# Top-32 attention into a mixture of experts: a drain planned anew between the last score tile and the first expert product

## The chip, the cores and the metric

One core of one Trainium2 chip runs the whole program. The metric is device microseconds of one execution; lower is better. Before the change the median of three runs is 365.16 us (362.47 to 365.77).

## The reference

```python
scores = scale * q @ k.T                      # 2 batches, 8 heads, 576 tokens, width 64
kth    = 32nd largest of each row
attn   = softmax(scores where scores >= kth, else -1e9) @ v
x      = attn as (1152, 512)                  # N = 1152 tokens
logits = x @ w_gate                           # 8 experts
e, gate_w = argmax(logits), softmax(logits)[e]
# each expert takes its tokens in order, up to its capacity of 288
out    = gate_w * (relu(x @ w1[e]) @ w2[e])   # 512 -> 1024 -> 512, a row of each token
```

## The kernel before

**Units.** The attention goes over 36 units u = 0 to 35: unit u = 4t + p is pair p of heads (two heads) of tile t of 128 tokens; there are nine tiles, t = 0 to 8. In the code L = 35 is the last unit and T = 8 the last tile. `attention` (L1041) is a pipeline written out by hand: in pass i it runs `heads(i)`, and steps of older units at fixed distances behind it.

**Steps of one unit.** `scores` (L292, PE) writes the scores into three PSUM banks. `heads` (L310, VectorE, called DVE) takes the eight largest of each of 16 segments, `merge` joins them, and `bound` (L346 to L350, three short DVE operations that depend on one another) makes a threshold from them. `shift` (L356, ScalarE, called ACT) copies the scores to SBUF. `sign` (L365, ACT) marks what is above the bound and counts it; `turn` (L372, mostly GpSimd, called POOL) multiplies the marks in; `select` (L393 to L400, DVE) finds the 32nd value; `penalty` (L409 ACT, L411 DVE) makes what is below it very small; `probs` (L428, L429 on PE, the exponential L430 on ACT) transposes and exponentiates; `values` (L450, L453, PE) multiplies by v; `normalise` (L464 to L469, DVE) divides, for two units at a time.

**Routing of a tile.** `route(t, stage)`: stage 0 transposes x (L516), 0.5 copies it out of PSUM (L520, L522), 1 makes the logits (L525), 1.5 splits x in two 16-bit halves (L528 to L534), 2, 2.1, 2.2 copy the logits (L536), find the largest and its index, 3 counts places (L545, L546), 3.5, 4, 5 work out slot and weight, 5.5 writes the tokens to `xbuf` in HBM by an indirect DMA of POOL (L559). The last tile has its stages 0 to 1 in two halves (0, 0.5, 1 and 0.1, 0.6, 1.1).

**Experts during the attention.** The first 128 tokens of the two experts first chosen ("a" and "b") are computed ahead. For "a" the hidden layer comes in four `quarter_h` (L657) with `quarter_take` (L704) and `quarter_split` (L708, L709), and the second product in four `quarter`s: each makes 128 of the 512 output columns with 24 matmuls (L757) and copies them out (L720). `split_w` cuts float32 weights in a 16-bit high part (part 0 or 2, L612, L616) and a low part (part 1, L618). Weights and loads live in 13 rotating SBUF buffers; one is taken again when the last reader of its tile is done.

**The drain.** After pass 34, L1124 to L1237 list by hand what is left, one list for all engines: each engine works through its own entries in that order, and waits where one is not ready. After the tokens of tile 8 are in `xbuf`, SyncE (called SP) loads them by transposing DMAs: `load_rest` (L648, L651) the rest of "a" and "b", `load_x(2)`, `load_x(3)` (L640) the next two experts. Then `experts` (L902) runs `ffn_rest` (first products L773) and the other six experts. Weights of 1 MB a piece are loaded by `load_w` (L603) on the same SP queue as the tokens; the scatters go through POOL's software queue.

Of the kernel before, what the change touches and what calls it, by code (L numbers as in the profile page):

```python
# [34 lines left out]
def kernel(  # L35
# [339 lines left out]
    def sign_turn(u, act, pool, turns=True):  # L375
        sign(u, (0,))
        for f, *a in act:
            f(*a)
        sign(u, (1,))
        if turns:  # L380
            turn(u, js=(0,))
        for f, *a in pool:
            f(*a)
        if turns:
            turn(u, js=(1,))
# [27 lines left out]
    def probs(u, *steps):  # L413
# [5 lines left out]
        for step in (0,) if whole else steps:  # L419
            if whole:  # L420
                bs, pt = range(9), P["p3", 0].tile([128, 9, 128], FT, name="p3", bufs=1)
            elif step < 2:
                bs, pt = range(5 * step, 5 * step + 4), bank4()
            else:
                bs, pt = (4,), (pv if TAIL_P else P["pt", 0].tile([128, 512], FT, name="ex", bufs=1))[:, None, 384:512]
# [269 lines left out]
    def quarter_h(c, a):  # L695
        if a == 0:
            Q["p"] = bank4()
        h_of(Q["p"][:, a], 0, 2 * c + a, "a")
# [12 lines left out]
    def quarter_y(c, a):  # L711
        if a == 0:
            Q["p"] = bank4()
        for k in (0, 1) if a == 0 else (2, 3):
            small_y("a", 0, Q["p"][:, 0], slice(128 * c, 128 * c + 128), k < 2, k % 2)

    def quarter_out(c):
        if c == 0:
            Q["y"] = work.tile([128, Dm], FT, name="y", tag="nat", bufs=4)
        nc.scalar.activation(Q["y"][:, 128 * c:128 * c + 128], Q["p"][:, 0], AF.Copy, scale=XE["a"][:, 0, 0:1])  # L720

    def quarter(c):
        quarter_y(c, 0)
        quarter_y(c, 1)
        quarter_out(c)
# [274 lines left out]
    def check(step):  # L1000
        if step == 1:
            pf = bank1()
# [14 lines left out]
    def count():  # L1017
        pc = bank1()
# [28 lines left out]
    def attention(side, early, late, mid, pads, act, pool, end):  # L1047
# [5 lines left out]
        for i in range(NU - 1):  # L1053
# [46 lines left out]
            run(at(4, values, 0) + picks + at(-1, scores) + at(4, values, 1) + routes((1, 1.5, 3)) + routes((0, 3.5)))  # L1100
# [8 lines left out]
            if last:  # L1109
                values(i - 3)  # L1110
# [20 lines left out]

        penalty(L - 3)
        bound(L - 1, 0)
        select(L - 2, 0)
        bound(L - 1, 1)
        select(L - 2, 1)
        bound(L - 1, 2)
        select(L - 2, 2)
        sign_turn(L - 1, act.get(L, []), [], False)
        run(pool.get(L, []))  # L1140
        probs(L - 3, 0, 1, 2)
        pad = [(lambda: None,)]
        small += [(select, L - 2, 3), (select, L - 2, 4)] + rt(T - 2, 2.1) + pad + rt(T - 2, 2.2) + [(turn, L - 1)]
        small += [(penalty, L - 2, (0,))] + 2 * pad + [(normalise, L - 4, st) for st in range(3)]
        heads(L, fill)
        drop()
        run(side.get(L, []))
        shift(L)
        penalty(L - 2, (1,))
# [6 lines left out]
        probs(L - 2, 0, 1, 2)  # L1156
        for st in range(3):
            bound(L, st)
        sign(L)
        run(rt(T - 2, 4))  # L1160
        quarter(0)
        values(L - 2)
        seq(select, L - 1, steps=(0, 1, 2, 3))
        run(rt(T - 2, 5))
        select(L - 1, 4)
        run(rt(T - 1, 0.5, 1))
        turn(L, (nc.gpsimd, nc.vector))
        for half in range(2):
            split_w(1, 1, 0, half, nc.gpsimd, 0)
        run(rt(T - 2, 5.5))  # L1170
        run(rt(T - 1, 1.5))
        penalty(L - 1)
        probs(L - 1, 0, 1, 2)
        seq(select, L, steps=(0, 1, 2))
        normalise(L - 2, 0)
        select(L, 3)
        normalise(L - 2, 1)
        select(L, 4)
        normalise(L - 2, 2)
        penalty(L, engs=(nc.vector, nc.scalar))  # L1180
        run(rt(T - 1, 2, 2.1, 2.2))
        for half in range(2):
            split_w(1, 1, 0, half, nc.vector, 1)
        load_w(2, 1, 0)
        for st in range(2, 9):
            pick(3, st)
        quarter(1)
        probs(L, 0, 1, 2)
# [5 lines left out]
        split_w(1, 1, 1, 0, nc.vector, 1)  # L1194
        quarter(2)
        run(rt(T, 0, 0.5))
        values(L)
        run(rt(T, 1))
        quarter(3)
        quarter_scatter()  # L1200
        seq(normalise, L, steps=(0, 1, 2))
        split_w(1, 1, 1, 1, nc.vector, 1)
        load_w(2, 1, 1)
        close_pool("att")
        open_pool("exp")
        for g in range(2):
            load_w(3, 0, g, True)
        run(rt(T, 0.1))
        small_h("b", 1, 0, first=TAIL_P[2].rearrange("p (c t) -> p c t", c=4))
        run(rt(T, 0.6, 1.1, 1.5))  # L1210
        small_h("b", 1, 1)
        run(rt(T, 2.1, 2.2, 3))
        small_h("b", 1, 2)
        run(rt(T, 3.5, 4, 5, 5.5))
        for f in range(3, KF):
# [6 lines left out]
        load_rest([nc.sync.value_load(row[:, e:e + 1], min_val=0, max_val=(E - 1) * cap + 128) for e in range(2)])  # L1222
        load_x(2, 0, SIZES[2])
        for g in range(2):
# [191 lines left out]
```

## Time and profile before

| | before |
|---|---|
| median of 3 runs | 365.16 us (362.47 to 365.77) |
| profiled execution | 364.38 us, of which its span is 362.6 us |
| TensorE clock granted over the span | 0.978 |
| busy: PE, DVE, ACT, POOL | 319.3, 305.5, 283.2, 238.9 us |
| DMA moved | 60.25 MB, mean 166 GB/s |

Three stages matter: up to about 218 us all engines are full with the pipeline of the attention; the drain reaches from the last scores (218.25) to the first product of `ffn_rest` (263.83); from there the experts run to the end. Times in the rows are from the start of the span; the time outside it is 1.8 us.

### The profile page before, as it was taken

The numbers are of one execution on the slowest core, as the hardware profiler recorded it, in microseconds if no ns is written. First come the engines' busy times: TensorE is split into PE (matmuls) and PEld (weight loads), VectorE is DVE, ScalarE is ACT, GpSimd is POOL, SyncE is SP. The second block draws the span as 40 slices with busy tenths as digits, with TensorE's granted clock in tenths as the row PEclk, the third lists the DMA queues.
The fourth block names the chain that finished last, engine by engine and source line by source line (L and its number), as shares of the span: only waits on it lengthen the run. The fifth ranks groups of instructions, "written<-read, shape, count | busy, mean of one in ns | idle before, by whom it ended". The sixth has DMA issues, their size and how long they took to land. (4 is left out here: it accounts for less than half of the span.)

```text
span 362.6 us, 9845 instructions
## 1 busy us (share of the span) xinstructions
PE 319.3 (88%) x3378; PEld 264.9 (73%) x3381; DVE 305.5 (84%) x1605; ACT 283.2 (78%) x498; POOL 238.9 (66%) x274
## 2 busy tenths in 40 slices
PE   6747888898888988989789999989789999999991
PEld 3535776787777876868588888989346999996681
DVE  5879999999999999999999996596626859799940
ACT  5879999999989999899899996762336847786820
POOL 3967979699894998999999989974011010219421
PEclk9888999999999999999899999999989999999998
DMA  9749897964485800000304524527579999997100
GB/s 168 129 106 208 201 217 211 221 150 101 100 281 193 309 3 31 4 0 32 116 3 129 200 82 125 216 98 247 214 213 343 316 392 308 322 381 169 59 25 24
DMA packets 69922, 60.25 MB, mean 166 GB/s; under 512 B 52070, under 2 KB 52070, under 8 KB 69864
## 3 DMA queue, kind: packets, MB, share of 16 engines
q1 hardware_dynamic: 67719, 54.79, 54.7%
q0 software_dynamic: 1616, 4.73, 3.6%
q8 instruction: 28, 0.46, 0.5%
q14 instruction: 31, 0.25, 0.2%
q10 hardware_dynamic: 528, 0.02, 0.1%
HBM read 40.66 MB, written 12.09 MB: 145 GB/s over the span
## 5 line engine op out<-in xcount | busy, mean ns | idle before, releaser
L310 DVE MAX8 un<-s 128x8 f32<-128x72 f32 (+2 forms) x576 | 102.1, 225 | 1.8 <-PE s L292 1.8
L372 POOL TENSOR_TENSOR z<-sm,sg 128x576 f32<-128x576 f32 x71 | 89.4, 1280 | 12.7 <-ACT sg L365 10.6
L677 POOL DMA_INDIRECT out_dram<-y,xp x12 | 24.4, 2033 | 82.8 <-DVE y L853 40.2
L453 PEld LDWEIGHTS pV<-vm,pT 128*128 128x128 f32 (+1 forms) x640 | 72.2, 183 | 6.9 <-issue 3.6
L453 PE MATMUL pV<-vm,pT 128*128 128x65 f32 (+1 forms) x640 | 73.3, 263 | 0.0
L618 DVE TENSOR_TENSOR ws<-wr,ws 128x1024 bf16<-128x1024 f32 x52 | 61.2, 1226 | 2.6 <-ACT ws L612 2.5
L356 ACT ACTIVATE sm<-s,mx 128x576 f32<-128x576 f32 (+2 forms) x108 | 54.7, 580 | 7.3 <-DVE mx L313 7.0
L365 ACT ACTIVATE sg<-sm,mx 128x576 bf16<-128x576 f32 x72 | 55.2, 770 | 5.8 <-POOL z L372 2.7
L292 PE MATMUL s<-qk 128*128 128x512 f16 (+3 forms) x320 | 45.4, 300 | 9.8 <-ACT sm L356 9.8
L428 PE MATMUL p<-ident,sm 128*128 128x128 f32 x252 | 48.3, 281 | 6.0 <-ACT xT L522 5.5
L409 ACT ACTIVATE pen<-sm,nk 128x576 bf16<-128x576 f32 x71 | 51.5, 775 | 1.8 <-DVE nk L400 1.3
L396 DVE MAX8 z<-z 128x8 f32<-128x576 f32 x72 | 51.0, 748 | 1.9 <-POOL z L372 1.9
L612 ACT ACTIVATE ws<-wr 128x2048 f16<-128x2048 f32 (+1 forms) x26 | 47.6, 1840 | 5.7 <-issue 4.4
L657 PEld LDWEIGHTS <-ws 128*128 128x128 f16 (+1 forms) x768 | 48.8, 98 | 0.9 <-issue 0.4
L429 PE MATMUL p<-identB,pen 128*128 128x128 bf16 x252 | 44.6, 220 | 3.5 <-ACT pen L409 3.4
L428 PEld LDWEIGHTS p<-ident,sm 128*128 128x128 f32 x252 | 36.1, 143 | 10.3 <-ACT xT L522 6.8
L429 PEld LDWEIGHTS <-pen 128*128 128x128 bf16 x324 | 33.5, 105 | 6.9 <-ACT pen L409 6.0
L292 PEld LDWEIGHTS <-qk 128*128 128x128 f16 (+1 forms) x320 | 20.8, 107 | 21.7 <-issue 13.8
L430 ACT ACTIVATE pT<-p 128x1152 f32<-128x1152 f32 x28 | 31.9, 1140 | 0.0
L618 POOL TENSOR_TENSOR ws<-wr,ws 128x1024 bf16<-128x1024 f32 x12 | 25.6, 2131 | 0.0
L838 PEld LDWEIGHTS <-ws 128*128 128x128 f16 (+1 forms) x288 | 21.3, 98 | 0.0
L657 PE MATMUL bk<-xe,ws 128*128 128x128 f16 (+7 forms) x312 | 21.1, 227 | 0.0
(276 smaller groups left out, 622.4 us busy)
## 6 DMA issues: line engine op xcount, KB each, us to landing
wr<-in_moe_w_dram SPq DMA_DIRECT2D x32, 1024.0 KB, 6.1
xbuf<-zero SPq DMA_DIRECT2D x6, 771.0 KB, 5.8
qnat<-in_q_dram SPq DMA_DIRECT2D x16, 144.0 KB, 3.5
knat<-in_k_dram SPq DMA_DIRECT2D x16, 144.0 KB, 3.4
out_dram<-zero SPq DMA_DIRECT2D x3, 768.0 KB, 4.6
vm<-in_v_dram SPq DMA_DIRECT2D x16, 128.0 KB, 3.1
qk<-qk SPq DMA_DIRECT2D x14, 144.0 KB, 2.4
vt<-in_v_dram SPq DMA_DIRECT2D x4, 64.0 KB, 4.6
```

Source lines behind the costliest of these rows:

```text
L292: nc.tensor.matmul(PS[u][a][row:row + n, o:o + w], QK[b][2 * i][:, h, s:s + n], QK[b][1][:, h, c:c + w], start=(i == 0), stop=(i == 1))
L310: nc.vector.max(out=un[:, j, i], in_=segment(u, j, i))
L356: nc.scalar.activation(SM[u][:, j, o], i, AF.Identity, bias=VAL[u][0][:, 0, j:j + 1], scale=-1.0)
L365: nc.scalar.activation(SG[u][j], SM[u][:, j], AF.Sign, bias=VAL[u][0][:, 2, j:j + 1], scale=-(1.0 - 2.0 ** -20), accum_out=CNT[:, c:c + 1])
L372: engs[j].tensor_tensor(out=Z[u][:, j], in0=SM[u][:, j], in1=SG[u][j], op=OP.mult)
L396: nc.vector.max(out=z8[:, step - 1], in_=Z[u][:, step - 1])
L409: eng.activation(o, x, AF.Relu, bias=n)
L428: nc.tensor.matmul(pt[:, i], sm[:, cs], ident, start=True, stop=False, is_transpose=True)
L429: nc.tensor.matmul(pt[:, i], pen[:, cs], identB, start=False, stop=True)
L453: nc.tensor.matmul(PV[t][row:row + n, h0 + half], PT[u][:, 5 * half + c, row:row + n], VM[b][:, c, p, half], start=False, stop=(half == 1 ...
L618: eng.tensor_tensor(out=w[:, 1].bitcast(BF)[:, s], in0=r[:, s], in1=w[:, 0, s], op=OP.subtract)
L657: nc.tensor.matmul(o, a(i), c(i), start=(i == 0 and m == 0), stop=(i == k - 1 and m == 2))
```

## The change

The list of the drain is written anew; nothing of what is computed changes. In parts:

1. The logits' copy of tile 6 (stage 2) leaves pass 34 and goes in among the last segments of `heads(35)`, which itself comes behind `bound(34)`, `sign(34)` and `turn(34)`. Only the first operation of `select(33)` stays among the segments.
2. `values(31)`, `normalise(31)`, `select(33)`, the splitting of tile 6 (1.5) and `quarter_h(3)` are put elsewhere; `select(34)`, `turn(35)`, `penalty(34)`, `select(35)` follow one another at once. `quarter_split(2)` waits for both `turn(33)`.
3. The split of the weight half (1,0,1) leaves POOL (two high and two low halves in passes 33 to 35); ACT makes its high part in one piece in the drain, DVE its low part.
4. `normalise(33)` stands ahead of the weight splits of DVE.
5. The second product of "a" is one over 512 columns in four steps `quarter_y` (8, 8, 4 and 4 matmuls), with one copy out; its scatter goes behind that of tile 8's tokens.
6. `load_w(2,1,1)` and the loads of expert 3 go behind the tokens' loads in SP's queue; `load_w(2,1,0)` goes behind `values(35)`.
7. PSUM: the transposes of tiles 7 and 8 share one bank (`TAIL_P[0]`), "a" has `TAIL_P[2]`, the last block of `probs` goes to `TAIL_P[3]`.

The diff, cut to its core (in the list of the drain removed and added lines are mixed as the diff has them):

```diff
     def sign_turn(u, act, pool):
...
+        turn(u, js=(0,))
+        if u < NU - 3:
+            for f, *a in pool:
+                f(*a)
+        turn(u, js=(1,))
+        if u == NU - 3:
+            for f, *a in pool:
+                f(*a)
...
-                px = TAIL_P[3 * (t % 2)].rearrange("p (c t) -> p c t", c=4)
+                px = TAIL_P[0].rearrange("p (c t) -> p c t", c=4)
...
+    def quarter_y(c):
+        small_y("a", 0, TAIL_P[2], slice(0, Dm), c < 2, c % 2)
+
+    def quarter_out():
+        Q["y"] = work.tile([128, Dm], FT, name="y", tag="nat", bufs=4)
+        nc.scalar.activation(Q["y"], TAIL_P[2], AF.Copy, scale=XE["a"][:, 0, 0:1])
...
-            if last:
-                small += [(route, NT - 3, 2, nc.gpsimd)]
...
-            if last:
-                values(i - 3)
...
+        for st in range(3):
+            bound(L - 1, st)
+        sign(L - 1)
+        turn(L - 1)
+        run(rt(T - 2, 1.5))
+        run(side.get(L, []))
+        small += [(select, L - 2, 0)] + 9 * pad + rt(T - 2, 2) + pad + rt(T - 2, 2.1) + pad
         heads(L, fill)
         drop()
+        values(L - 4)
         shift(L)
+        probs(L - 3, 0, 1, 2)
+        select(L - 2, 1)
+        select(L - 2, 2)
+        small += [(select, L - 2, 3)] + rt(T - 2, 2.2) + [(select, L - 2, 4)] + [(normalise, L - 4, st) for st in range(3)]
         merge(L, fill)
+        drop()
+        for st in range(3):
+            bound(L, st)
         swap_psum("sc", "bk")
         tail_p()
+        penalty(L - 2)
+        quarter_h(3, 0)
+        quarter_h(3, 1)
         values(L - 3)
         run(rt(T - 2, 3, 3.5))
+        sign(L)
+        seq(select, L - 1, steps=(0, 1, 2, 3, 4))
+        run(rt(T - 2, 4))
+        turn(L, (nc.gpsimd, nc.vector))
+        penalty(L - 1)
+        probs(L - 2, 0, 1, 2)
         run(rt(T - 1, 0))
+        seq(select, L, steps=(0, 1, 2, 3))
+        run(rt(T - 2, 5))
+        select(L, 4)
+        penalty(L, engs=(nc.vector, nc.scalar))
+        run(rt(T - 1, 0.5))
+        quarter_take(3)
+        run(rt(T - 2, 5.5))
+        probs(L - 1, 0, 1, 2)
         values(L - 2)
         for half in range(2):
             split_w(1, 1, 0, half, nc.gpsimd, 0)
+        quarter_split(3)
+        run(rt(T - 1, 1, 1.5))
+        split_w(1, 0, 1, None, nc.scalar, 2)
+        probs(L, 0, 1, 2)
+        seq(normalise, L - 2, steps=(0, 1, 2))
         run(rt(T - 1, 2, 2.1, 2.2))
+        for c in (0, 1):
+            for half in range(2):
+                split_w(1, 1 - c, c, half, nc.vector, 1)
+        quarter_y(0)
         values(L - 1)
         run(rt(T - 1, 3, 3.5))
         for half in range(2):
             split_w(1, 1, 1, half, nc.scalar, 2)
         run(rt(T - 1, 4, 5, 5.5))
+        for st in range(2, 9):
+            pick(3, st)
         run(rt(T, 0, 0.5))
         values(L)
+        load_w(2, 1, 0)
         run(rt(T, 1))
         seq(normalise, L, steps=(0, 1, 2))
+        split_w(1, 1, 1, 0, nc.vector, 1)
+        quarter_y(1)
...
         run(rt(T, 0.1))
+        quarter_y(2)
         run(rt(T, 0.6, 1.1, 1.5))
+        quarter_y(3)
+        quarter_out()
+        small_h("b", 1, 0)
+        run(rt(T, 2.1, 2.2))
         small_h("b", 1, 1)
+        run(rt(T, 3, 3.5, 4, 5, 5.5))
+        split_w(1, 1, 1, 1, nc.vector, 1)
+        quarter_scatter()
...
+        load_rest([nc.sync.value_load(row[:, e:e + 1], min_val=0, max_val=(E - 1) * cap + 128) for e in range(2)])
+        load_w(2, 1, 1)
+        load_x(2, 0, SIZES[2])
+        for g in range(4):
+            load_w(3, g // 2, g % 2, True)
+        load_x(3, 0, SIZES[3])
         check(0)
         check(1)
         count()
...
-    halves = [(e, i, c) for e, i, c in ((0, 0, 0), (0, 0, 1), (0, 1, 0), (0, 1, 1), (1, 0, 0), (1, 0, 1))]
+    halves = [(e, i, c) for e, i, c in ((0, 0, 0), (0, 0, 1), (0, 1, 0), (0, 1, 1), (1, 0, 0))]
...
-    for c in range(4):
+    for c in range(3):
         end[31 + c] = [(quarter_h, c, 0), (quarter_h, c, 1)]
```

## Rows read from the trace of the kernel before

**Rows 1.** Chain that ended last, in order of time: start us, us, what.
```profile
274.44 3.65 PE pT L761 x32
...
325.95 2.68 PE pT L657 x48
```
**Rows 2.** Stretches: length; busy PE, PEld, DVE, ACT, POOL; PE's clock, DMA share, GB/s.
```profile
219.95:263.83 43.88, 38.25 (x436) 33.19 (x437) 30.85 (x137) 24.22 (x49) 26.68 (x32) 1.00 0.54 181
...
264.00:266.00 2.00, 2.00 (x16) 0.88 (x14) 2.00 (x2) 0.23 (x1) 1.26 (x1) 0.69 0.12 14
266.00:268.00 2.00, 2.00 (x12) 0.84 (x10) 0.05 (x1) 0.00 (x0) 0.00 (x0) 0.50 1.05 216
268.00:270.00 2.00, 2.00 (x20) 1.05 (x18) 0.00 (x0) 0.60 (x1) 0.00 (x0) 0.96 1.03 334
...
310.00:320.00 10.00, 10.00 (x157) 9.96 (x155) 7.95 (x11) 8.55 (x8) 2.01 (x2) 1.00 1.12 315
```
**Rows 3.** Waits of PE from 219.95 to 263.9: total us, times, longest.
```profile
PE bk L773 <- DMA xe<-xbuf: 2.3, 2, 1.4
PE pV L450 <- DVE xr L469: 0.8, 1, 0.8
PE pV L450 <- ACT pT L430: 0.7, 1, 0.7
PE pT L429 <- DVE r L536: 0.6, 1, 0.6
```
**Rows 4.** Timeline of DVE: start us, us, engine, line, what [idle before <-releaser].
```profile
220.13 0.17 DVE L536 COPY r<-pV 128x8 f32<-128x8 f32 x1 [2.69 <-PE pV L525]
...
222.96 0.22 DVE L310 MAX8 un<-s 128x8 f32<-128x72 f32 x1
...
228.05 0.16 DVE L350 TENSOR_TENSOR mx<-mx,pD 128x2 f32<-128x2 f32 x1
...
237.47 0.17 DVE L400 TENSOR_REDUCE nk<-ds 128x2 f32<-128x16 f32 x1
```
**Rows 5.** Timeline of POOL.
```profile
213.66 2.06 POOL L616 TENSOR_SCALAR ws<-wr 128x1024 f16<-128x1024 f32 x2
...
220.97 1.27 POOL L372 TENSOR_TENSOR z<-sm,sg 128x576 f32<-128x576 f32 x1
...
228.07 2.52 POOL L372 TENSOR_TENSOR z<-sm,sg 128x576 f32<-128x576 f32 x2
...
252.96 1.00 POOL L559 DMA_INDIRECT xbuf<-xs,ru  x1 [1.66 <-DVE ck L1009]
```
**Rows 6.** Timeline of ACT.
```profile
221.70 0.78 ACT L365 ACTIVATE sg<-sm,mx 128x576 bf16<-128x576 f32 x1 [2.62 <-DVE mx L350]
...
274.28 1.91 ACT L612 ACTIVATE ws<-wr 128x2048 f16<-128x2048 f32 x1
```
**Rows 7.** Timeline of PE.
```profile
230.20 1.06 PE L757 MATMUL pT<-ws,hh 128*128 128x128 f16 x16
...
231.54 0.44 PE L450 MATMUL pV<-vt,pT 128*128 128x130 f32 x2
...
255.76 3.62 PE L757 MATMUL pT<-ws,hh 128*128 128x512 f16 x15 [0.34 <-DVE cm L1024]
259.21 1.89 PE L757 MATMUL pT<-ws,hl 128*128 128x512 f16 x8
...
263.83 7.05 PE L773 MATMUL bk<-ws,xe 128*64 128x512 f16 x47 [0.97 <-DMA xe<-xbuf]
```
**Rows 8.** SP's queue: start us, us, line, what, count.
```profile
246.63 1.66 SPq L603 DMA_DIRECT2D wr<-in_moe_w_dram  x3
...
259.71 2.57 SPq L648 DMA_TRANSPOSE xe<-xbuf  x2
```
**Rows 9.** To landing: L559's scatters by line; weight loads from the page's DMA issues.
```profile
DMA to landing us min/median/max: 3.0/3.1/3.4
...
wr<-in_moe_w_dram SPq DMA_DIRECT2D x32, 1024.0 KB, 6.1
```

More of the change, by code (lines that the diff above doesn't have):

```diff
@@ L379, in sign_turn @@
         sign(u, (1,))
[L380 to L385, printed above, removed]
+        turn(u, js=(0,))
[6 more added lines that the diff above has]
+                f(*a)
     def select(u, step, scale=-1.0):
@@ L424, in probs @@
             else:
-                bs, pt = (4,), (pv if TAIL_P else P["pt", 0].tile([128, 512], FT, name="ex", bufs=1))[:, None, 384:512]
+                bs, pt = (4,), (TAIL_P[3] if TAIL_P else P["pt", 0].tile([128, 512], FT, name="ex", bufs=1))[:, None, 384:512]
             for i, c in enumerate(bs):
@@ L709, in quarter_split @@
         nc.gpsimd.tensor_tensor(out=hl, in0=Q["r"], in1=hh, op=OP.subtract)
[L711 to L725, printed above, removed]
+    def quarter_y(c):
[3 more added lines that the diff above has]
+        nc.scalar.activation(Q["y"], TAIL_P[2], AF.Copy, scale=XE["a"][:, 0, 0:1])
     def quarter_scatter():
@@ L1099, in attention @@
             picks = at(2, select, 1) + at(2, select, 2) + at(0, merge, None, 0)
-            run(at(4, values, 0) + picks + at(-1, scores) + at(4, values, 1) + routes((1, 1.5, 3)) + routes((0, 3.5)))
+            run(at(4, values, 0) + picks + at(-1, scores) + at(4, values, 1) + routes((1, 3) if last else (1, 1.5, 3)))
+            run(routes((0, 3.5)))
             run(mid.get(i, []))
             small += at(2, select, 3) + at(2, select, 4)
-            if last:
-                small += [(route, NT - 3, 2, nc.gpsimd)]
             run(at(0, merge, fill, 1))
@@ L1129, in rt @@
             return [(route, t, st, nc.vector if t >= T - 1 else nc.gpsimd) for st in stages]
+        pad = [(lambda: None,)]
         penalty(L - 3)
[L1133 to L1143, printed above, removed]
@@ L1157, in attention @@
[L1157 to L1161, printed above, removed]
-        values(L - 2)
[L1163 to L1167, printed above, removed]
+        sign(L)
[4 more added lines that the diff above has]
+        probs(L - 2, 0, 1, 2)
@@ L1174, in attention @@
[L1174 to L1180, printed above, removed]
-        run(rt(T - 1, 2, 2.1, 2.2))
[L1182 to L1188, printed above, removed]
+        quarter_split(3)
+        run(rt(T - 1, 1, 1.5))
@@ L1193, in attention @@
         run(rt(T - 1, 4, 5, 5.5))
-        split_w(1, 1, 1, 0, nc.vector, 1)
-        quarter(2)
+        for st in range(2, 9):
+            pick(3, st)
         run(rt(T, 0, 0.5))
         values(L)
+        load_w(2, 1, 0)
         run(rt(T, 1))
-        quarter(3)
-        quarter_scatter()
         seq(normalise, L, steps=(0, 1, 2))
-        split_w(1, 1, 1, 1, nc.vector, 1)
-        load_w(2, 1, 1)
+        split_w(1, 1, 1, 0, nc.vector, 1)
+        quarter_y(1)
         close_pool("att")
         open_pool("exp")
-        for g in range(2):
-            load_w(3, 0, g, True)
         run(rt(T, 0.1))
-        small_h("b", 1, 0, first=TAIL_P[2].rearrange("p (c t) -> p c t", c=4))
+        quarter_y(2)
         run(rt(T, 0.6, 1.1, 1.5))
+        quarter_y(3)
+        quarter_out()
+        small_h("b", 1, 0)
+        run(rt(T, 2.1, 2.2))
         small_h("b", 1, 1)
[L1212 to L1215, printed above, removed]
+        run(rt(T, 3, 3.5, 4, 5, 5.5))
+        split_w(1, 1, 1, 1, nc.vector, 1)
+        quarter_scatter()
+        for f in range(2, KF):
             small_h("b", 1, f)
@@ L1221, in attention @@
         count()
-        load_rest([nc.sync.value_load(row[:, e:e + 1], min_val=0, max_val=(E - 1) * cap + 128) for e in range(2)])
-        load_x(2, 0, SIZES[2])
-        for g in range(2):
-            load_w(3, 1, g, True)
-        load_x(3, 0, SIZES[3])
         small_low("b", 0)
@@ L1231, in attention @@
         split(2, 1, 2)
-        o = bank1()
+        o = TAIL_P[3]
         for high in (True, False):
```

16 lines of the change are left out of this document (4 added, 12 removed).

## The prediction

> **What bounds the kernel now.** I read the chain that ended last first. From 274.44 us on each of its pieces is PE's, one behind the other, up to 329 us [rows 1]: the experts hold PE without a gap, so whatever lets `ffn_rest` start earlier moves the end by as much, as long as weights keep up. Then I read the stretch ahead of it, 219.95 to 263.83, the drain. It lasts 43.88 us, and PE is busy for 38.25 of them [rows 2]. The difference, 5.63 us, is all that better order can win in the drain; the rest is work of PE that stays. The waits of PE say where it lies: 2.3 us for the tokens of `ffn_rest`, 0.8 for a normalisation, 0.7 for an exponential, 0.6 for a penalty [rows 3], and about 1.2 in pieces of 0.2 to 0.3. Last I read the other engines' timelines, to see what is late behind each wait.
>
> DVE has nothing to do from 217.44 to 220.13: it waits 2.69 us for the logits of tile 6, with `bound(34)` queued behind the copy [rows 4]. ACT therefore waits 2.62 us and starts `sign(34)` at 221.70 [rows 6]. DVE starts `heads(35)` at 222.96, ends `bound(35)` at 228.21, and has the result of `select(35)` at 237.64 [rows 4]. POOL is late as well: two weight halves from 213.66 hold it 2.06 us, `turn(33)` ends at 222.24 and `turn(34)` runs only from 228.07 to 230.59 [rows 5].
>
> The tokens have their own chain. The last scatter starts on POOL at 252.96 [rows 5]; the transposing loads that wait for it leave at 259.71 [rows 8], 6.75 us later, where the scatters whose landing the trace gives (the last is not among them) took 3.0 to 3.4 us from issue to landing [rows 9]. Three weight loads of 1 MB left SP at 246.63 [rows 8].
>
> **The change, part by part.**
>
> *Bound ahead of the copy.* `bound(34)` runs at 217.5 and costs 0.6 us (three operations of 0.16 with a hop between them) [rows 4]. `heads(35)` starts at 218.1, 4.9 us earlier. The copy stands behind eleven of sixteen segments; at 0.22 us a segment [rows 4], of which some 0.07 overlap by my estimate, it comes up between 219.9 and 220.5, the logits are there at 220.1, so 0.2 us is left of the 2.69. Behind it on DVE stand the last five segments only. `sign(34)` goes to about 219.1, as soon as ACT has the penalty of unit 32 behind it.
>
> *POOL freed.* Without the halves at 213.66 `turn(33)` ends near 219.2, `quarter_split(2)` follows, and `turn(34)` runs at 220.3 to 222.8 in place of 228.07 to 230.59. The same work elsewhere: ACT gets 1.9 us in one piece (one such piece took 1.91 [rows 6]) ahead of `exps(35)`, while PE has `values(33)`, logits and `probs(35)` to do; DVE gets two more low halves, some 1.2 to 1.4 us each, ahead of the last tile's routing. If DVE's cover is gone, `normalise(35)` is late: I make it 242.9 instead of 242.1. Behind it on PE stand the transposes of tile 8, but `quarter_y(1)` is ahead of them for 1.7 us, so it costs nothing; without that cover, 0.8 us.
>
> *The chain of unit 35.* `heads` ends at 221.4, `select(33)` and `merge` with what is put in between at 224.2, `normalise(31)` at 225.0, `bound(35)` at 225.6 (228.21 before), `sign(35)` 226.1 to 227.9, `turn(35)` 228.8, `select(35)` 230.7 (237.64 before). Seven microseconds earlier, it no longer decides: PE gets to `probs(35)` only at about 234. So PE's wait for the penalty (0.6) goes. The wait for the exponential (0.7) goes too, since `quarter_y(0)` and `values(34)` stand between. The wait for `normalise(31)` (0.8) shrinks to about 0.3. One is new: `exps(33)` moves behind `penalty(34)` on ACT, and `probs(34)` needs the two banks that it empties; PE waits some 0.8 us there.
>
> *Product over 512 columns.* Four quarters took 1.34 us each, 230.20 to 231.54 [rows 7], 5.36 in all. 24 products over 512 columns take 3.45 us for the sixteen from 255.76 to 259.21 and 1.7 for the eight behind [rows 7], 5.2 in all: 0.2 us won. Three copies of ACT fall away, off the path. Both steps ahead of the last tile's places, `quarter_y(2)` and `(3)`, last as long as the quarters they replace.
>
> *Weights behind tokens.* The scatter's start moves with PE by what is saved ahead of it, some 2 us, to 251.0. If it lands in 3.1 us, it is there at 254.1; the first transposed tokens reach PE 4.1 us after the loads leave (259.71 to 263.83 [rows 7, 8]), at 258.2. PE has work up to 259.6 by the sum below, so the tokens' wait of 2.3 us goes, with 1.4 us to spare. The scatter of "a" now stands behind that of the tokens in POOL's queue and meets nothing. What is late now: `load_w(2,1,1)` leaves SP after four token loads, near 258.5, and lands after 6.1 us [rows 9], at 264.6; ACT wants it at 274.28 before [rows 6], so at 268.7. The four pieces of expert 3 are wanted a good six microseconds later still. This costs nothing, if DMA keeps its pace; the bounds are 0 and the 7.8 us of the third rival.
>
> *Clock.* PE stands idle for most of 261 to 263.8, and its granted clock then falls: 0.50 from 266 to 268, with 12 products in 2 us, 0.96 in the next two, with 20 [rows 2]. 0.50 is the lower level, 1.2 GHz. The 47 products of `ffn_rest` took 7.05 us [rows 7]; at the pace of 268 to 270, some 0.11 us each when the one or two that reach in are left out, they take 5.2. Bounds are 0 and 1.8; with the idle time gone I take 1.5.
>
> *Sum.* Waits left in the drain: 0.3 + 0.8 + about 0.6 for the count behind `check` (bank and copies, small pieces as before) = 1.7. Won: 5.63 - 1.7 + 0.2 = 4.1 ahead of `ffn_rest` (start 259.7), and 1.5 in it: 5.6. The profiled execution took 364.38, its span 362.6: 364.4 - 5.6 = 358.8. It lies 0.8 below the median of the runs shown, 365.16, well inside their spread of 3.3, and I forecast from it.
>
> **Rivals.**
>
> *The scatter lands late whoever is ahead.* The 6.75 us from the scatter to the loads may not be the weights' doing. Then the scatter from 251.0 is answered at 257.7, the tokens are on PE at 261.9, PE waits 2.2 us again and its clock falls: 1.9 us is won, 362.5. For it: no view says what held its packets. Against it: the scatters that met no such queue of loads took 3.0 to 3.4 us [rows 9]. The Trainium skill (DMA: Bandwidth & Descriptors, Queues, rings and completion order) says that each DMA engine goes round its queues packet by packet; by that rule weights on SP's queue would not hold a scatter of POOL's queue behind all of them, and the move would win little. The trace speaks rather against it, with 6.75 us beside 3.1, but not firmly.
>
> *The waits come back elsewhere.* ACT from 219 to 236 is then nearly full, and the order by hand is strict: one late piece (the ACT split, or DVE's four low halves) is passed on to PE. If half of the 4.1 goes so, and the clock still falls, 2.1 is won: 362.3; if all, 364.4.
>
> *Weights are late (slower).* DMA is full in the experts' stage, 1.12 of its engines' time and 315 GB/s from 310 to 320 [rows 2]. Three more MB now come into this stage: at 400 GB/s some 7.8 us of transfers. As long as pieces land before their splits, that shows nowhere. From the point at which the backlog is larger than the lead of the loads over the splits, PE waits for all of it: 358.8 + 7.8 = 366.6. Against it: the tokens leave 5.6 us earlier, so do the loads behind them, and between 259 and 266 DMA had hardly anything to do (a share of 0.12 from 264 to 266 [rows 2]). A smaller form: `load_w(2,1,1)` lands 6 us later than its median, and PE loses 2 us.
>
> *No effect.* That would need PE's waits to be something other than what the view names; the 5.63 us bound of the drain leaves no larger win either.
>
> **How the numbers follow.** Forecast, 355.5 to 361.4: 0.62. Late scatter, 361 to 363: 0.14. Waits elsewhere, 362 to 364.5: 0.15. Late weights, 364.5 to 369: 0.09. The lower end is a start-to-start count of the drain (which leaves out the tails of matmuls that the busy time has in it and gives 1 us more), the whole 1.8 of the clock, and a fast draw of runs as 362.47 was one. The range 355.5 to 364.0 leaves out the slower case and little beside. About 1% is what can be told from no change here, 3.65 us: faster holds for nearly all of the first case (0.61), and some of the second and third (0.07): 0.68. Within 1%: 0.25. Slower: 0.07.
>
> **What would show it.** Right: `heads(35)` begins near 218.1 and `bound(35)` ends near 225.6; `turn(34)` runs from 220.3; PE's busy time from its logits of tile 6 to `ffn_rest` is still 38 us in a stretch of some 40; `ffn_rest` begins near 259.7 with no wait for tokens, its 48 products take about 5.2 us, the granted clock stays near 1; the token loads leave some 3 us after the scatter starts; the experts behind it last as long as before. Wrong: a wait for tokens above 1 us at `ffn_rest`, a granted clock near 0.5 behind it, ACT waiting for a weight piece in the first two experts, or PE waiting more than 2 us in the drain for exponentials or normalisations.

## The result, and the profile after

The changed kernel takes 359.01 us (median, 358.36 to 360.87) where the kernel before, on the same chip, took 364.94: a ratio of 0.986 (95% interval 0.982 to 0.990). A ratio counts only executions within 1.5% of the fastest of the same kernel, which leaves out one run of part 6 alone (366.36 us) and two of the four quarters (367.73 and 368.78). Two more groups of runs gave 359.25 and 359.88 us, with ratios of 0.985 and 0.986. The forecast was 358.8 in a range of 355.5 to 364.0, and faster. The profiled execution took 358.36 us with a span of 356.5; before it was 364.38 and 362.6.

The rows below answer rows shown of before. Lines have moved: the copy of the logits is L538 now (L536), the first products of `ffn_rest` are L766 (L773), `small_y` is L750 (L757), weight loads are L605 (L603), the token loads that transpose L650 (L648), the scatters L561 (L559), the splits L614 and L620 (L612 and, for the low halves, L618).

Stretches of after: length; busy PE, PEld, DVE, ACT, POOL; PE's clock, DMA share, GB/s. The first answers the drain of [rows 2].

```profile
219.60:258.80 39.20, 37.59 (x367) 30.31 (x368) 32.82 (x123) 21.86 (x44) 21.49 (x28) 1.00 0.40 122
...
264.00:266.00 2.00, 1.87 (x16) 1.20 (x16) 0.74 (x2) 1.83 (x3) 0.00 (x0) 1.00 1.88 104
266.00:268.00 2.00, 1.67 (x18) 0.69 (x14) 0.41 (x2) 2.00 (x3) 0.00 (x0) 1.00 0.96 340
```

The drain lasts 39.20 us instead of 43.88. PE waits 1.61 us in it instead of 5.63. Behind it, from 264 to 268, the clock stays at 1.00 where it had fallen to 0.69 and 0.50. The waits that are left, of after's PE in this stretch (us in total, times, longest; compare [rows 3]):

```profile
PE bk L527 <- DVE r L553: 0.5, 1, 0.5
PE bk L996 <- DVE fl L1007: 0.3, 1, 0.3
PE pV L452 <- DVE r L538: 0.3, 1, 0.3
PE bk L1012 <- DVE flags L997: 0.2, 1, 0.2
PE pT L430 <- ACT pT L432: 0.2, 1, 0.2
```

None of the four waits of [rows 3] is among them. Timelines of after show the other engines (start us, us, engine, line, what, [idle before <- releaser]), DVE first, then POOL and PE:

```profile
219.92 0.17 DVE L538 COPY r<-pV 128x8 f32<-128x8 f32 x1 [0.29 <-PE pV L527]
...
224.72 0.16 DVE L350 TENSOR_TENSOR mx<-mx,pD 128x2 f32<-128x2 f32 x1
...
220.18 2.52 POOL L372 TENSOR_TENSOR z<-sm,sg 128x576 f32<-128x576 f32 x2
...
250.54 1.21 POOL L561 DMA_INDIRECT xbuf<-xs,ru  x1 [3.35 <-DVE ru L560]
...
258.73 5.37 PE L766 MATMUL bk<-ws,xe 128*64 128x512 f16 x48
```

The copy waits 0.29 us where it had waited 2.69 [rows 4]; the bound of unit 35 ends at 224.88 (228.21); `turn(34)` runs at 220.18 (228.07 [rows 5]); the scatter starts at 250.54 (252.96), and the 48 products of `ffn_rest` follow the work before them without a wait and take 5.37 us, where 47 took 7.05 [rows 7]. SP's queue of after shows why there is no wait:

```profile
244.48 0.39 SPq L605 DMA_DIRECT2D wr<-in_moe_w_dram  x1
253.94 2.58 SPq L650 DMA_TRANSPOSE xe<-xbuf  x2
...
258.27 0.40 SPq L605 DMA_DIRECT2D wr<-in_moe_w_dram  x1
...
262.43 2.79 SPq L605 DMA_DIRECT2D wr<-in_moe_w_dram  x4
```

The token loads leave 3.40 us after the scatter starts; before it was 6.75 [rows 5, 8].

So what follows `ffn_rest`'s first products on PE starts at 264.03 instead of 270.82, 6.8 us earlier. But the span is shorter by 6.1 only. The missing 0.7 us is at the far end. This is the chain that ended last, of after:

```profile
320.37 12.03 DMA wr<-in_moe_w_dram
...
332.42 1.91 ACT ws L614
334.33 0.49 ACT hh L734
...
334.87 3.63 PE bk L750 x16
```

A load of the last group of weights left at 320.37 and took 12.03 us, twice the median of before [rows 9]; ACT splits it late, and PE waits 0.7 us for ACT. In before the chain was PE's own up to 329 [rows 1]; behind that it too runs over ACT's splits, but no load stands in it, and PE waits for nothing from 300 on. The same place of before:

```profile
334.48 3.70 ACT ws L612 x2
338.18 0.48 ACT hh L741
...
341.01 3.63 PE bk L757 x16
```

Not only is PE earlier, the weights are later: from 332 to 333 us after still moves 0.39 MB, before only 0.06, although PE is 6.8 us ahead in after. Part 6 put 3 MB of loads from ahead of the tokens behind them.

### The profile page after: what moved, and what is told of

Same layout as the page of the kernel before. It is cut to its first block, busy times and chain, and to the rows that moved or that the text cites. A ratio compares the mean times of both kernels' runs of the same rounds, so it can differ in the third digit from the quotient of the medians.

```text
span 356.5 us, 9708 instructions
## 1 busy us (share of the span) xinstructions
PE 314.8 (88%) x3309; PEld 259.6 (73%) x3309; DVE 310.9 (87%) x1607; ACT 283.2 (79%) x496; POOL 233.6 (66%) x270
## 5 line engine op out<-in xcount | busy, mean ns | idle before, releaser
L455 PEld LDWEIGHTS pV<-vm,pT 128*128 128x128 f32 (+1 forms) x640 | 71.3, 181 | 6.7 <-issue 3.3
L455 PE MATMUL pV<-vm,pT 128*128 128x65 f32 (+1 forms) x640 | 72.4, 261 | 0.0
L620 DVE TENSOR_TENSOR ws<-wr,ws 128x1024 bf16<-128x1024 f32 x54 | 64.8, 1251 | 2.7 <-ACT ws L614 2.5
L614 ACT ACTIVATE ws<-wr 128x2048 f16<-128x2048 f32 (+1 forms) x27 | 49.6, 1845 | 7.6 <-issue 4.9
L292 PE MATMUL s<-qk 128*128 128x512 f16 (+3 forms) x320 | 43.9, 294 | 8.7 <-ACT sm L356 8.6
L430 PEld LDWEIGHTS p<-ident,sm 128*128 128x128 f32 x252 | 36.2, 144 | 10.5 <-ACT xT L524 6.8
L620 POOL TENSOR_TENSOR ws<-wr,ws 128x1024 bf16<-128x1024 f32 x10 | 21.4, 2138 | 0.0
L659 PE MATMUL pT<-xe,ws 128*128 128x128 f16 (+5 forms) x312 | 19.6, 222 | 0.0
```

Source lines behind the costliest of these rows:

```text
L292: nc.tensor.matmul(PS[u][a][row:row + n, o:o + w], QK[b][2 * i][:, h, s:s + n], QK[b][1][:, h, c:c + w], start=(i == 0), stop=(i == 1))
L430: nc.tensor.matmul(pt[:, i], sm[:, cs], ident, start=True, stop=False, is_transpose=True)
L455: nc.tensor.matmul(PV[t][row:row + n, h0 + half], PT[u][:, 5 * half + c, row:row + n], VM[b][:, c, p, half], start=False, stop=(half == 1 ...
L614: nc.scalar.activation(w[:, 0, s], r[:, s], AF.Copy)
L620: eng.tensor_tensor(out=w[:, 1].bitcast(BF)[:, s], in0=r[:, s], in1=w[:, 0, s], op=OP.subtract)
L659: nc.tensor.matmul(o, a(i), c(i), start=(i == 0 and m == 0), stop=(i == k - 1 and m == 2))
```

## The experiments

Each is a kernel that differs by the few lines shown, in a comparison with the kernel before on the same chip. "After" is the changed kernel. Five undo one part of it, one does one part alone, and two go further. Parts 2 and 7 were not undone by themselves.

### Part 6 undone: weights ahead of the tokens

```diff
+        load_w(2, 1, 1)
         ...
+        for g in range(2):
+            load_w(3, 0, g, True)
         ...
-        load_w(2, 1, 1)
         ...
-        for g in range(4):
-            load_w(3, g // 2, g % 2, True)
+        for g in range(2):
+            load_w(3, 1, g, True)
```

> The changed kernel with its part 6 undone: load_w(2,1,1) and the first two pieces of expert 3 stand ahead of the token loads again. Theory (weights hold the scatter up): the scatter starts near 250.5 as in the changed kernel, the token loads leave some 6.5 us later (3.4 in the changed kernel), PE is ready at 258.7 and waits about 2.5 us for tokens, its granted clock falls behind that, the 48 products of ffn_rest take near 7 us in place of 5.3; weights of the last experts come earlier, which gives back up to 0.7: about 362.4 us. Rival (the scatter shares the DMA engines packet by packet and is not held up by loads): the token loads leave 3.4 us after the scatter, no wait, clock near 1: 358.3 to 359.

Measured: 362.18 us, ratio to before 0.990 (0.987 to 0.993). POOL's scatter starts at 250.44, the loads of the tokens leave at 257.42, 7.0 us later. Waits, a stretch and PE's timeline of this kernel:

```profile
PE bk L766 <- DMA xe<-xbuf: 2.1, 2, 1.9
...
262.00:264.00 2.00, 2.00 (x12) 0.84 (x10) 1.98 (x2) 0.57 (x1) 1.16 (x1) 0.53 0.20 32
...
261.58 7.05 PE L766 MATMUL bk<-ws,xe 128*64 128x512 f16 x47 [0.15 <-DMA xe<-xbuf]
```

The wait is back with its 2.1 us, behind it the clock falls to 0.53, and the products take 7.05 us again, to the hundredth what before had [rows 7]. Part 6 is worth 2 to 3 us beside the rest (after itself was not run beside it), and the clock is a large part of it: the products alone take 1.7 us more. The rival that the scatter is late in any case has fallen: nothing but the loads ahead of it is different, and it takes 7.0 us instead of 3.4. The DMA view by stretches of 1 us shows whose packets moved, first from 254 to 255, then from 256 to 257 (queue: packets, MB, share of the engines' time; q1 has SP's loads, q0 POOL's scatters):

```profile
q1 hardware_dynamic: 91, 0.32, 100.8%
q0 software_dynamic: 1, 0.00, 1.0%
...
q1 hardware_dynamic: 65, 0.26, 63.7%
q0 software_dynamic: 58, 0.17, 42.8%
```

From the scatter's start until 254.5 no packet of POOL's queue moves; its first ones come 4.1 to 4.6 us behind the start, where in after, with DMA empty, they came 1.5 to 2.0 behind. From 255 on the two queues move side by side, and the tokens' loads leave at 257.42 while weights still move. So some 2.6 of the 3.6 us lie ahead of the scatter's first packet.

The Trainium skill (DMA: Bandwidth & Descriptors, Queues, rings and completion order) says that a DMA engine takes its queues in turn, packet by packet. The trace agrees from 255 on; what held the first packets until then no run here shows. To count on a small transfer getting through would have been wrong by 3.6 us.

### Part 6 alone, on the kernel before

```diff
-        load_w(2, 1, 1)
         ...
-        for g in range(2):
-            load_w(3, 0, g, True)
         ...
+        load_w(2, 1, 1)
         ...
-        for g in range(2):
-            load_w(3, 1, g, True)
+        for g in range(4):
+            load_w(3, g // 2, g % 2, True)
```

> The kernel before with part 6 alone: load_w(2,1,1) and all four pieces of expert 3 go behind the token loads; the drain is as before. Theory: the token loads leave some 3.4 us after the scatter of 252.96, at 256.4 in place of 259.71; the tokens are there at 260.5, PE has work to 261.1 and does not wait; the clock stays near 1, ffn_rest's products take 5.3 in place of 7.0 and end at 266.4 in place of 270.82: 4.4 us won, of which late weights in the last experts may take back up to 1: 360.5 to 361.5. Rival (scatter late in any case): 364 to 365, or worse by the weights that now come later.

Measured: 363.88 us, ratio 0.995 (0.990 to 0.999), outside the 360.5 to 361.5 expected. The profiled run, 360.09, shows what the theory names (no wait for tokens, clock 1.00, first product at 261.24), but of ten runs four lay between 360.09 and 361.97 and six between 363.76 and 366.36. Over the whole span the six had no lower granted clock (0.965 to 0.982) than the four (0.968 to 0.982). A second profile was to say why:

> The kernel before with part 6 alone, looked at once more, since its runs lay between 360.1 and 366.4 and only one of 360.1 has been seen in a profile. Theory: the later runs have the clock's fall in the drain that the first look had not: TensorE's windows of the drain show a granted clock under 0.9 somewhere between 220 and 262, and the first product over the token columns starts later than 261.2 by as much as the time is longer. Rival: the drain is the same and the difference lies behind 275.

It took 361.81, so it is not one of the six. Its drain is not slower: the clock is 1.00 throughout and the first product starts at 260.09, 1.15 us ahead of the first profile. The theory that the clock does it falls here. These are PE's waits and a stretch of the second profile:

```profile
PE bk L757 <- ACT hh L741: 2.1, 1, 2.1
PE bk L657 <- DMA xe<-xbuf: 0.4, 1, 0.4
...
330.00:340.00 10.00, 7.88 (x87) 5.44 (x85) 8.27 (x9) 6.88 (x6) 3.73 (x3) 1.00 1.12 285
```

PE loses 2.5 us behind 330 for late weights and tokens, with DMA full (1.12); the first profile has no such wait of PE. What the drain wins, the last experts can give back, and how much differs from run to run. Whether the six slower runs are more of the same no profile shows.

### Part 4 undone: normalisation behind the splits

```diff
-        seq(normalise, L - 2, steps=(0, 1, 2))
         run(rt(T - 1, 2, 2.1, 2.2))
         for c in (0, 1):
             for half in range(2):
                 split_w(1, 1 - c, c, half, nc.vector, 1)
+        seq(normalise, L - 2, steps=(0, 1, 2))
```

> The changed kernel with part 4 undone: normalise(33) stands behind the four weight splits of DVE. Theory (values(34) needs the bank that normalise(33) empties, so DVE's order is on PE's path): normalise(33) ends near 242.2 in place of 234.1, PE waits some 5 us ahead of values(34), ffn_rest starts 4 to 5 us later: 363 to 364. Rival (PE has enough other work there, or the order of DVE does not matter): 359.

Measured: 370.04 us, ratio 1.013 (1.006 to 1.021): slower than before. Waits of PE and stretches of this kernel:

```profile
PE pV L452 <- DVE xr L471: 5.2, 1, 5.2
...
236.00:240.00 4.00, 1.56 (x8) 0.49 (x5) 4.00 (x4) 2.54 (x7) 3.92 (x4) 1.00 0.00 0
240.00:244.00 4.00, 1.20 (x6) 1.20 (x6) 2.68 (x4) 0.40 (x1) 0.92 (x1) 0.57 0.00 0
244.00:248.00 4.00, 4.00 (x22) 4.00 (x22) 0.94 (x10) 0.38 (x1) 0.00 (x0) 0.50 0.00 0
248.00:252.00 4.00, 4.00 (x21) 3.93 (x21) 1.54 (x10) 0.00 (x0) 1.17 (x2) 0.50 0.47 102
```

The wait was sized right, 5.2 us, the price was not: 363 to 364 us was expected, and the first product comes at 269.24, 10.5 us late. Behind the idle time PE works at or near the lower level, 1.2 GHz (0.50 to 0.57), in the three stretches from 240 to 252, although it is busy in two of them from end to end; the next one still has 0.73. A step of 0.8 us in DVE's order decides over 11 us.

### The logits' copy back in pass 34

```diff
+            if last:
+                small += [(route, NT - 3, 2, nc.gpsimd)]
         ...
-        small += [(select, L - 2, 0)] + 9 * pad + rt(T - 2, 2) + pad + rt(T - 2, 2.1) + pad
+        small += [(select, L - 2, 0)] + 9 * pad + pad + pad + rt(T - 2, 2.1) + pad
```

> The changed kernel with part 1's copy undone: the copy of tile 6's logits goes back to pass 34, where VectorE waits for TensorE's logits. Theory: VectorE waits 2.7 us again near 217, the heads' work of unit 35 starts near 220.2 instead of 217.8, its bound ends near 227.2, and since unit 35's chain still feeds TensorE, the first product over the token columns starts 2.3 us later, near 261: 361.3 to 361.6 us. Rival: the chain of unit 35 has slack by now, the wait is there and the first product stays within 0.5 us of 258.7: 359 to 359.5 us.

Measured: 360.76 us, ratio 0.989 (0.986 to 0.993). DVE's and PE's timelines of this kernel:

```profile
220.14 0.17 DVE L538 COPY r<-pV 128x8 f32<-128x8 f32 x1 [2.70 <-PE pV L527]
...
227.21 0.16 DVE L350 TENSOR_TENSOR mx<-mx,pD 128x2 f32<-128x2 f32 x1
...
261.14 3.21 PE L766 MATMUL bk<-ws,xe 128*64 128x512 f16 x28
```

DVE's wait of 2.70 us is back, the bound of unit 35 ends 2.5 us later, and the first product starts 2.4 us later, as the theory had it (the view ends at 264, within the 48 products). The rival (slack hides it) has fallen. The time rose by 1.5 us beside after on the same chip, less than the 2.3 expected, and lies below the 361.3 to 361.6 forecast. Of the 2.4 us some 0.5 is another wait, PE's for the flags (L997), which takes 0.7 here and 0.2 in the first profile of after; the first product of after itself stood at 258.73, 259.23 and 260.35 in three profiles (below), so two profiles can differ by more than the medians. The way to PE is not the one the expectation named: PE waits 1.0 us ahead of a product of `values`, and the profile names the bound's first operation, which ends on DVE together with `normalise(31)` ahead of it, at 226.9. That is the wait of 0.8 us in [rows 3]; the copy had caused it.

### The split back on POOL

```diff
-        split_w(1, 0, 1, None, nc.scalar, 2)
         ...
-        for c in (0, 1):
-            for half in range(2):
-                split_w(1, 1 - c, c, half, nc.vector, 1)
+        for half in range(2):
+            split_w(1, 1, 0, half, nc.vector, 1)
         ...
-    halves = [(e, i, c) for e, i, c in ((0, 0, 0), (0, 0, 1), (0, 1, 0), (0, 1, 1), (1, 0, 0))]
+    halves = [(e, i, c) for e, i, c in ((0, 0, 0), (0, 0, 1), (0, 1, 0), (0, 1, 1), (1, 0, 0), (1, 0, 1))]
```

> The changed kernel with part 2's first half undone: GpSimd takes the split of expert 4's second half in passes 33 to 35 again, and ACT and VectorE no longer do it. Theory: the turn of pass 33 ends near 221.1 on GpSimd and that of pass 34 near 226.9, 4 us later than without, the one-hot work of tile 6 behind them near 231.7, and TensorE waits some 4.7 us in sum where tile 6 needs it, with the clock's fall on top: 363.7 to 366 us. Rival: ACT and VectorE are relieved by as much and the drain is bound by them: 360 us or less.

Measured: 364.63 us, ratio 1.000 (0.997 to 1.003): with this one part undone, all that the change won is gone. Waits, POOL's timeline and a stretch of this kernel:

```profile
PE pV L547 <- POOL oh L545: 2.7, 1, 2.7
...
224.15 2.52 POOL L372 TENSOR_TENSOR z<-sm,sg 128x576 f32<-128x576 f32 x2
...
232.00:236.00 4.00, 4.00 (x29) 3.16 (x27) 3.07 (x8) 3.32 (x8) 2.45 (x4) 0.57 0.00 0
```

(The expectation calls this part 2's first half; it is part 3.) `turn(34)` starts 4.0 us later on POOL. The one-hot of tile 6 (L545, which marks each token's expert) stands behind it and, now, behind a low half of 2.1 us too; it runs at 231.06 instead of 225.02, and PE waits 2.7 us for it, not 4.7; the clock then stands at 0.57 from 232 to 236, as it did behind the other waits. The first product comes at 263.85. The rival, that ACT and DVE would give the time back, has fallen.

### Four quarters in place of the product over 512 columns

```diff
     def quarter_y(c):
-        small_y("a", 0, TAIL_P[2], slice(0, Dm), c < 2, c % 2)
+        cols = slice(128 * c, 128 * c + 128)
+        for k in range(4):
+            small_y("a", 0, TAIL_P[2][:, cols], cols, k < 2, k % 2)
```

> The changed kernel with part 5 undone: tile 7's expert product again in four quarters, each a product over fewer columns, in the place of the halves over 512 columns. Theory: four times 1.34 us instead of 1.89 + 1.89 + 1.03 + 1.02 less the overlaps (5.2 us net), 0.2 us more on TensorE, and at most as much again from where the quarters stand: 359.0 to 359.6 us where the changed kernel has 359.1, which can't be told from it in time; the sum of the product's rows tells it. Rival: the quarters fill gaps that the halves leave, and the first product over the token columns comes 0.3 us earlier, at 258.4 or before.

Measured: 361.57, 365.20, 367.73 and 368.78 us; the ratio's rule leaves the first two, of which one was profiled (365.20). They lie far apart, but the fastest is slower than the slowest of sixteen runs of after (360.87). The expectation missed. PE's timeline of this kernel, around the second half of the last tile's logits (L527):

```profile
246.62 1.06 PE L752 MATMUL bk<-ws,hh 128*128 128x128 f16 x16
247.51 0.61 PE L752 MATMUL bk<-ws,hl 128*128 128x128 f16 x8
247.96 0.56 PE L527 MATMUL bk<-wg,xT 128*128 128x8 f32 x4
...
262.56 5.37 PE L768 MATMUL bk<-ws,xe 128*64 128x512 f16 x47 [0.16 <-DMA xe<-xbuf]
```

The same place in a profile of after that had the same fall of the clock near 222 (the second of the three told of below):

```profile
245.98 1.03 PE L750 MATMUL bk<-ws,hl 128*128 128x512 f16 x4
246.84 0.51 PE L527 MATMUL bk<-wg,xT 128*128 128x8 f32 x4
247.21 1.02 PE L750 MATMUL bk<-ws,hl 128*128 128x512 f16 x4
```

The quarters take 1.34 us each as predicted. But the two forms put different shares into the late steps. After does eight and eight matmuls early (1.89 us each) and leaves four and four (1.03 and 1.02 with their ends) for the last two steps; the quarters leave 1.34 and 1.34. The logits' second half comes 1.1 us later (247.96 to 246.84), the scatter 1.65 (253.33 to 251.68), and the first product 1.65 (262.00 to 260.35). PE was 0.65 us behind ahead of the first quarter already (tile 7's logits at 234.91 and 234.26), so 1.0 us is the quarters' own: the two late steps take 1.34 us each from start to start, where after's take 0.86. The two early steps are shorter instead, but that wins nothing, since PE then waits for unit 35's normalisation (0.5 us here, 0.8 in this profile of after). Not the sum of the product counted, but what of it stands behind that wait and ahead of the last scatter. Another 0.56 us goes behind the first product: the tokens' loads leave 4.27 us after the scatter, where after's leave 3.21 after it, and 47 of the 48 products start only at 262.56. Why the loads leave later was not tried.

The rest of the loss is at the end: PE waits there 2.6 us for expert weights; the load in its chain lands at 338.17, where that of after's first profile landed at 332.39. One group of four loads left SP at 284.15, where that profile's left at 278.24, so 5.9 us later behind a drain that was 3.3 us later. What held that group was not tried, and how the slowest runs come to 368.78 stays open.

### Two versions that go further, and after beside them

The first takes the last weights of expert 2 earlier: `load_w(2, 1, 0)` ahead of the routes' stage `pick(3)`, `load_w(2, 1, 1)` behind `values(35)`.

```diff
+        load_w(2, 1, 0)
         for st in range(2, 9):
             pick(3, st)
         ...
-        load_w(2, 1, 0)
+        load_w(2, 1, 1)
         ...
-        load_w(2, 1, 1)
```

> The changed kernel with load_w(2,1,0) one step earlier, ahead of pick(3), and load_w(2,1,1) behind values(35) in place of behind the token loads; expert 3 stays behind the tokens. Theory (in the changed kernel the DMA backlog makes the weights of expert 7 late, PE waits 0.7 us for their splits; and DMA has room from 240 to 250): the two loads leave near 242, are through by 249, the token loads still leave 3.4 to 4 us after the scatter, the last piece of expert 7 lands 2.5 us earlier and the wait goes: 358.2 to 358.6. Rival (two loads there hold the scatter up as three did): token loads leave later, 360 or more.

Measured: 358.94 us, ratio 0.982 (0.976 to 0.987). The wait for weights at the end is gone and the scatter is not held (3.5 us), but the median is above the 358.2 to 358.6 expected and within the runs of after, of which none was made beside it. What the earlier loads alone are worth is therefore not shown. The second takes two orders more: the fourth of DVE's splits goes behind tile 7's stages 4 to 5.5, and `normalise(35)` ahead of `pick(3)`.

```diff
-        for c in (0, 1):
-            for half in range(2):
-                split_w(1, 1 - c, c, half, nc.vector, 1)
+        for i, c, half in ((1, 0, 0), (1, 0, 1), (0, 1, 0)):
+            split_w(1, i, c, half, nc.vector, 1)
         ...
         run(rt(T - 1, 4, 5, 5.5))
-        for st in range(2, 9):
-            pick(3, st)
+        split_w(1, 0, 1, 1, nc.vector, 1)
+        load_w(2, 1, 0)
         run(rt(T, 0, 0.5))
         values(L)
-        load_w(2, 1, 0)
+        load_w(2, 1, 1)
         run(rt(T, 1))
         seq(normalise, L, steps=(0, 1, 2))
+        for st in range(2, 9):
+            pick(3, st)
```

> The changed kernel with three orders more: unit 35's normalisation goes ahead of the stage that picks the routes, the last of VectorE's four splits goes behind stages 4 and 5 of token tile 7, and the last loads of weights go out earlier (one ahead of the routes' stage, one behind unit 35's values). Theory: the 0.5 us that TensorE waits in the bank of the last logits goes, the normalisation ends about 1 us earlier, and the wait for expert 7's weights at the end (0.7 us of the path) goes: 358.2 to 358.5 where the changed kernel has 359.0, and no weight wait above 0.3 us behind 330. Rival: the DMA engines are full from 260 to 332 in either order, so what is earlier for one weight is later for another, and the two kernels can't be told apart.

> The changed kernel once more, beside the others of this group: 359.0 us (358.4 to 360.9 so far), and in its profile the first product over the token columns at 258.7 and a wait of 1 to 1.5 us for expert 7's last weights near 331.

Measured: 357.71 us, ratio 0.982 (0.978 to 0.985), beside 359.25 for after on the same chip. The expectation for after missed: its profile here had the first product at 260.35 and no wait for weights (below). Both were run once more on another chip:

> The kernel with the three orders more once again, beside the changed kernel: 357.7 us against 359.1, so 1.0 to 1.8 us ahead if its gain is in the kernel; if the first group's 357.7 was an accident of the clock, 358.5 to 359.5.

> The changed kernel beside it: 359.1 us (358.4 to 360.9). In its profile either no fall of the clock behind 222 and a wait for expert 7's weights at the end, or the fall (some 1.2 us) and no such wait.

Measured: 357.39 (ratio 0.979, 0.976 to 0.982) beside 359.88 for after. So this version is 1.5 to 2.5 us ahead of after, more than the 0.5 to 0.8 expected at first. Its profile has neither the wait of 0.5 us ahead of the last tile's logits (L527) nor one for weights behind 300; unit 35 is normalised at 243.1 instead of 244.5, and the chain at the end is PE's and ACT's own:

```profile
327.30 3.70 ACT ws L614 x2
331.00 0.49 ACT hh L734
...
333.82 3.63 PE bk L750 x16
```

These products start 1.05 us ahead of those of after's first profile (334.87). But that profile waited only 0.2 us for the flags (L997); this version waits 0.7, and so does the third profile of after, whose products start at 335.19. Beside that one the version is 1.4 us ahead, near the lower difference of the medians, 1.5. Where the 2.5 us on the other chip come from I can't say.

The three profiles of after are not alike. From 222 to 224, after's first profile:

```profile
222.00:224.00 2.00, 2.00 (x27) 1.89 (x26) 1.93 (x18) 1.39 (x3) 1.92 (x4) 1.00 0.85 326
```

The same two microseconds in its second profile:

```profile
222.00:224.00 2.00, 2.00 (x16) 1.67 (x16) 1.93 (x18) 0.92 (x2) 1.92 (x4) 0.56 0.73 258
```

There the granted clock is at or near its lower level for some 4 us (0.56 and 0.58). The product of `ffn_rest` comes 1.6 us later (260.35), and the wait for weights at the end is not there; the span is 0.9 us longer, not 1.6. The third has no fall and loses 0.6 us at the end, like the first, but its first product stands at 259.23, 0.5 us later, since PE waits longer for the flags:

```profile
PE bk L1012 <- DVE flags L997: 0.8, 1, 0.8
```

The second has 0.7 there. So of its 1.6 us some 1.1 belong to the fall, and the first profile's 0.2 is the exception among the three.

## Why the prediction was right, step by step

*The drain.* Right in place and size. Forecast were 1.7 us of waits left, and 1.61 are; 3.9 of 5.63 us were to go by the order, and 4.0 went. That close a match is partly luck: in the two other profiles of after, with 0.5 us more for the flags, some 2.2 us are left and 3.4 went. Of the single waits two were misjudged. The 0.8 us for the banks that `exps(33)` empties are 0.2. The 0.3 for `normalise(31)` is not in the list; in its place PE waits 0.3 us for the logits' copy, L538, ahead of `values(31)`, which writes the same PSUM bank. And 0.5 us are new: the last tile's logits wait for stage 4 of tile 7, whose logits are in the same bank (`TAIL_P[1]`) and which stands on DVE behind four low halves. I had these at 1.2 to 1.4 us each; the four take 6.49 in a row, 1.6 each, while single ones later take 1.22. The undone copy and the undone split show that DVE's wait and POOL's halves held the chain.

*Unit 35.* `heads(35)` begins at 217.77 (forecast 218.1), `bound(35)` ends at 224.88 (225.6), the result of `select(35)` is there at 231.3 (230.7). Unit 35 is normalised at 244.5 (242.9), mostly since the splits ahead are longer. With the normalisation of unit 33 behind them PE would have waited 5.2 us.

*The product over 512 columns.* Right in its sum, and undersized in effect: I counted 0.2 us of PE's time, and the statement that the two last steps "last as long as the quarters they replace" was wrong. They last 0.86 us each from start to start instead of 1.34, and they stand ahead of the last scatter, so by the two profiles compared the part is worth 1.0 us there.

*Weights behind tokens.* Right: 3.4 us from scatter to loads (forecast 3.1), no wait at `ffn_rest`. The chance of 0.14 for the late scatter was given to something that the undone part excludes. The prediction says that no view tells what held the scatter's packets in before. The DMA view by half microseconds tells at least when they moved: POOL's queue moves 0.27 MB from 253 to 256 (as much as the scatter of "a" ahead of it brings), nothing from 256 to 257, and the rest from 257.0 on, which I take for the tokens', 4.0 us behind their scatter's start.

*Clock.* 1.5 us were taken, with a bound of 1.8; the products take 5.37 instead of 7.05 us, so 1.7 were won, nearly the bound, as far as two profiles tell.

*Sum.* Ahead of the end of `ffn_rest`'s first products 6.8 us were won, where 5.6 were forecast: 4.0 of waits, 0.7 of PE's busy time (37.59 against 38.25; 0.2 was forecast, the ends of matmuls are modelled, so I take no more from it), 1.7 of clock, and 0.35 since the stretch begins earlier. 0.7 were lost behind 330. The step that was missing is this one: I looked for late weights in the first two experts and had a small form of 2 us there. They were late at the last expert. DMA is full from 260 to 330, 0.93 to 1.24 of its engines' time by stretches of 10 us, but in before it was full from 270 on as well; what is new is the 3 MB that now come into this stage, so that the transfers end some 3 us later while the work that needs them comes earlier. The rival of late weights had this mechanism and the 3 MB, and saw it as all or nothing. So 6.1 is left of 6.8; that 358.8 lies 0.2 us from the measured median is luck, since errors of 1.2 and 0.7 us nearly cancel.

*Not additive.* Undoing one part costs 1.5 (copy), 2 to 3 (weights), 5.4 (POOL's split) and 11 us (normalisation), some 20 in all, where the whole change wins 6. The new order stands or falls as one: each part moves work to where the next part has made room. A prediction that adds up parts is safe only if it walks through the order once, as a whole.

## What to carry to other kernels

Where one engine is to be kept busy, cost a wait twice: its length, and what the clock takes behind it (5.2 us of waiting cost 10.5; behind 2.1 us the products took 1.7 more). A small transfer on which the next stage waits goes out ahead of large ones, whichever queue they are on. And if the stage behind is full of transfers, time won ahead of it must be followed to the last of them: starting two loads earlier, in idle DMA time, took the wait at the end away, though only together with two more orders did the time fall clearly.

## What was unexpected of the hardware

The granted clock fell at 222 in the second profile of after, in that of the four quarters and in the second of the version with three orders more (0.50 from 222 to 224 in both), and not in the first of after, though in after's two PE was busy 1.46, 1.84 and 1.90 us of the three stretches of 2 us before it, and 1.46, 1.88 and 1.86 in the execution without a fall. So the same order of work can meet either level. Between executions that differ in it the first product is 1.1 to 1.5 us later where it happens (260.35 beside 259.23 of after's third, 259.64 beside 258.16 of the other version), and the span 0.3 to 1.1.

A load of 1 MB that landed in 6.1 us [rows 9] takes 12.03 at the end of after. A full DMA is not the reason by itself: the last four loads of before left 2.3 to 2.6 us apart, from 316.73 on, and those that the view gives landed in 6.1 to 6.2 us with DMA full as well (1.00 from 316 to 330). After's four left within 2 us, from 319.12 on, and took 8 to 12 (1.09 from 319 to 333). The time to landing tells how much is queued, here 4 MB. DVE's two-input split of 128x1024 takes 1.22 us when POOL has little to do and 1.6 on average in the row of four, beside which POOL is busy for 3.92 of 4 us (236 to 240). POOL's operations suffer too: the low part of a quarter (L711) takes 1.54 us there and 0.67 at 219.55, where DVE is at work as well, but on the largest-eight operation of `heads`. I had priced both by their rows elsewhere.
